# Memory attention with FFN: last quarter of the FFN for the first 384 tokens in float16 halves, later quarters in reverse order

## The chip, the cores and the metric

One core of a Trainium2 chip runs the whole program. The metric is device time in microseconds (us), lower is better; the time before is the median of three runs. A profile is one execution of its own, taken by the hardware profiler; its time is given beside them.

The engines named below are PE (TensorE, matrix products), DVE (VectorE), ACT (ScalarE), POOL (GpSimd) and SP (which issues nearly all transfers). PE reads SBUF and writes PSUM, a memory of eight banks here divided into three pools.

## The reference

Eight batches of eight heads, 576 positions, head size 64. A softmax of `phi` pools keys and values into 32 slots per head; the queries attend to these slots; the result, 4608 tokens of 512 numbers, goes through a feed-forward network (FFN) of width 2048 with a leaky ReLU.

```python
a = softmax(phi, over the 32 slots)               # b h s m
k_m = einsum('bhsm,bhsd->bhmd', a, k)
v_m = einsum('bhsm,bhsd->bhmd', a, v)
attn = softmax(q @ k_m.T / 8)                     # b h s m
x = (attn @ v_m) as (4608, 512)
h = x @ w_in                                      # 512 -> 2048
out = maximum(0.01 * h, h) @ w_out                # 2048 -> 512
```

## The kernel before

**Folding.** `attn @ v_m @ w_in` is computed as `attn @ (v_m @ w_in)`. For each batch b and each quarter j of the FFN's width (four quarters of 512), a fold multiplies the batch's `vT` with the quarter of `w_in` (L1007); the result is the weight of the up products of that batch. So all that PE streams for the FFN is the attention matrix `a` against folded weights (up), and the activated `g` against `w_out` (down).

**Float32 and halves.** A product of float32 operands is one matmul, which the profile shows as two instructions. In halves each operand is split into a float16 high part and a float16 remainder, and a product becomes three matmuls: high x high, remainder x high, high x remainder. The high part is made on ACT (or by a cast on DVE), the remainder by a subtraction on DVE or POOL. The weights arrive as 64-bit numbers and are first rebuilt as float32 (steps `ld`, `h`, `y`, `t`); their scales for halves are known only when all four quarters of `w_in` (`ci.1` to `ci.4`) and of `w_out` (`co.1` to `co.4`) have been squared and summed (`b`).

**Groups and units.** The first 1152 tokens (batches 0 and 1) are done in three groups of 384 tokens, each in eight units: unit u works on quarter u // 2, two blocks of 128 of it (i = 0, 1). A unit's steps are P (up products of a block, PE), V (leaky ReLU, ACT), C and L (the halves of g, DVE), and O (down products of a block into three PSUM tiles, PE). Group 0 (units `u0` to `u7`) runs wholly in float32, before the scales are known, and has no C and L. Groups 1 and 2 (units 8 to 15 and 16 to 23) run in halves. Tokens from 1152 on go through other functions (steps `p`, `v`, `s`, `c`, `l`, `d`, `x`, `z`), which the change doesn't touch.

**Order.** It is written out by hand: `OPENING` and `LATER` are lists of steps, and each step issues its instructions on one engine. On an engine they run in the order of the lists; between engines they wait for data and for buffers to come free. Names of steps used below:

- `a1.*` is the attention of batch 1: `C10` pools keys and values (PE), `C30`, `C31`, `C4` scale them (DVE), `C3k` (ACT), `D10` transposes the keys (PE), `D3` copies them (ACT), `D2` spreads a maximum (PE), `E1` the scores (PE), `E20` to `E22` transpose them (DVE), `Q0`, `Q1` transpose the queries (DVE). `Sc1` to `Sc8` are the softmax of chunk c and its halves, `S02`, `S05`, `S08`, `S12`, `S15`, `S18` of them on POOL.
- `a2.phi` loads phi of batch 2 (SP), `a2.A1` is its maximum and `a2.B10` the subtraction of it (DVE).
- `f0j.1`, `f0j.2`: fold of batch 0, quarter j, in float32 (PE), and its copy to SBUF (ACT). `Wbj.p`: fold for batch b (PE); `Wbj.h0`, `h1`, `l0`, `l1`: its high parts (ACT) and remainders (DVE).
- `oj.k`, `l`: halves of `w_out`, quarter j (ACT, DVE). `oj.s`, `m`, `n`: sums of its blocks for the tokens from 1152 on, and their halves (DVE, ACT, DVE). `ij.k`, `l`: halves of `w_in`.
- `Z0.t`: store of tile t of group 0. `e.`, `e2.`, `osb`: scales (DVE).

The PSUM pool `ps_a` has three banks for everything but the FFN, `ps_h` two for up products, `ps_o` three for down products. A fold takes two banks of `ps_a`, a `co` step one. A load takes the next of eight slots of a ring, or a fixed place, and waits on SP until the last reader of that place is done; what is behind it on SP waits too.

The lines that matter: up products L1091 to L1117, the leaky ReLU L1119, down products L1183 to L1200, stores L1167, folded weights L1042 to L1066, which weight lies in which buffer L309 to L315, the steps of group 0 L1359 to L1389.

Of the kernel before, what the change touches and what calls it, by code (L numbers as in the profile page):

```python
# [45 lines left out]
o1.ld1 u0.P1 a0.S17 i1.y0 o0.t1 u1.V1 i1.h0 i1.h1 i1.y1 i1.t1 u0.V1 i2.ld0 i1.y2 i1.h2 o1.y1 o1.y2
o1.t0 o1.h1 i1.t0 u1.O0 u0.O1 o1.h2 i2.ld1 o2.ld0 i1.t2 f01.1 i2.h0 i2.y0 i2.y1 a0.S18 i2.h1 i2.t1
i2.ld2 f01.2 o2.ld1 o1.t2 o2.ld2 o1.t1 u1.O1 i2.t0 u2.P1 o2.h0 u2.P0 i2.y2 i2.h2 a1.phi o2.y0 i2.t2
o2.t0 a1.kv1 a1.q0 a1.kv0 f02.1 u2.V0 u3.P1 u2.O0 o2.y1 o2.h1 o2.t1 a1.kv2 o2.y2 o2.h2 a1.kv3 a1.A1
u2.V1 u3.P0 o2.t2 i3.ld0 f02.2 a1.q1 a1.A2 a1.A3 u4.P1 a1.B0 u3.V1 u4.P0 a1.B10 u3.V0 i1.b u3.O0  # L50
i2.b u4.V0 a1.B20 u5.P0 a1.B3 o0.b a1.C10 i3.ld2 a1.Q0 i3.ld1 a1.C2 u5.V0 o1.b u2.O1 i3.y0 u5.P1
u4.V1 a1.C30 a1.C31 a1.C3k a1.C4 a1.D10 a1.D2 o2.b i3.h0 a1.D3 a1.Q1 i3.y2 i3.h2 a1.D11 a1.D4 u3.O1
i3.t2 a1.E1 o3.ld0 a1.D5 i3.y1 u4.O0 i3.h1 i3.t0 o3.h0 u5.V1 o3.y0 o3.ld2 u5.O0 a1.E20 i3.t1 a1.E21
i3.b ci.1 o3.ld1 a1.E22 f03.1 a1.S01 a1.S11 a1.S02 a1.S03 a1.S04 u4.O1 o3.y2 o3.y1 o3.h2 ci.2 o3.t0
f03.2 a1.S12 ci.3 ci.4 e. o3.h1 o3.t1 a1.S05 u6.P0 u6.V0 a1.S13 a1.S06 a1.S07 u6.P1 u7.P0 a1.S14
a1.S15 o3.t2 w0.2 u7.V0 u6.O0 a1.S16 o3.b w1.1 co.1 co.2 u7.O0 w1.2 co.3 u6.V1 co.4 u5.O1 o0.k0
# [16 lines left out]
P12.0 o1.m1 O10.0 C11 V12.0 o1.n1 L11 P12.1 o1.s2 O10.1 o1.m2 W03.l1 o1.s3 V12.1 W03.l0 a2.A3 o1.n2
o2.k0 C12 W13.p o2.k2 o2.l0 W13.h1 P13.0 W13.h0 W13.l1 P13.1 W13.l0 V13.0 o2.k1 L12 V13.1 O11.0
o1.m3 P14.0 o2.l1 V14.0 C13 o2.s0 P14.1 L13 o2.m0 O11.1 a2.B10 V14.1 o1.n3 o2.n0 o2.s1 P15.0 a2.B20
C14 o2.m1 O12.0 o2.s2 V15.0 o2.n1 o2.m2 a2.C10 L14 P15.1 o2.s3 a2.B3 O12.1 o2.l2 a2.q0 V15.1 o2.n2
o3.s0 a2.q1 o3.k1 o3.k0 o3.l1 P16.0 P16.1 o3.k2 O13.0 V16.0 C15 o2.m3 o3.s1 O13.1 V16.1 C16 o3.l0
o3.s2 o3.m1 a2.C2 a2.C30 i0.l1 o3.l2 o3.m2 P17.0 L15 o3.m3 o3.n3 O14.0 V17.0 L16 a3.phi P17.1 a2.Q0
# [6 lines left out]
O19.1 i3.k0 W22.p V22.1 a3.A1 i3.k2 L21 a3.A2 W22.h0 P23.0 W22.h1 O20.0 V23.0 a2.S07 P23.1 a3.A4
O20.1 V23.1 a2.S08 i3.l2 C22 i3.l0 W22.l1 C23 W21.l1 O21.0 i3.l1 L23 p0.0 W23.p v0.0 p0.1 W23.h0
p0.2 L22 a3.A3 W23.h1 a3.B10 O21.1 W22.l0 v0.1 a3.B20 W23.l1 a3.C10 O22.0 os2 a3.B3 v0.2 a3.q0
W23.l0 a4.phi a3.C2 p0.3 a3.C30 a3.q1 O22.1 v0.3 a3.C3k s0 c0.0 a3.C31 l0.0 c0.1 a3.D10 l0.1 p1.0
p1.1 a3.D11 v1.0 O23.0 v1.1 a3.C4 p1.2 p1.3 a3.D3 v1.2 a3.Q0 O23.1 v1.3 p2.0 Z2.0 Z2.1 s1 d0.0 Z2.2
p2.1 v2.0 d0.1 v2.1 a3.D2 a4.A1 a3.D4 c1.0 d0.2 c1.1 p2.2 l1.0 d0.3 v2.2 a3.D5 d0.4 a4.A2 p2.3 a4.A4  # L90
# [1403 lines left out]
```

## Time and profile before

| | us |
|---|---|
| median of 3 runs (lowest, highest) | 649.48 (649.35, 651.62) |
| time of the profiled execution | 647.19 |
| its span, first to last instruction | 645.3 |
| PE busy | 632.7 |
| DVE busy | 515.0 |
| ACT busy | 391.2 |
| POOL busy | 29.5 |

The span is what the engines' records cover; the rest of the execution's time lies before its first and after its last instruction. An engine's busy time is the union of its instructions. In a timeline row stand start, length, engine, line of the program, operation, tiles, shapes and count, and in brackets the idle time just before and what ended it; neighbours of one kind are merged. In a view by stretches there are, after the stretch and its length, the busy time of each engine with its number of instructions, the clock granted to TensorE, the DMA engines' busy share and GB/s. A group of instructions has its busy time and mean length in ns, then the idle time before its members. Stretches that matter here: the opening, to about 32 us; group 0, to about 103 us; groups 1 and 2, to about 214 us; the rest.

### The profile page before, as it was taken

To read this page: it belongs to the slowest core of one execution; us is meant where nothing else is said; L and a number is where in the kernel's file an instruction comes from. 1 tells how busy PE (TensorE), PEld (TensorE's weight loads), DVE (VectorE), ACT (ScalarE), POOL (GpSimd) and SP (SyncE) were. 2 spreads that over 40 slices of the span, in tenths; PEclk is the share of its full clock that TensorE was granted. 3 is DMA by queue.
4 is the path that set the end of the run, shared out by engine and by line. 5 is a ranking of instruction groups with operands and counts; after the bars stand their busy time and mean duration, and the time that the engine had idled before them with its cause. 6 is when DMAs were issued, how large, how long until landed. Compare 5 with 4: busy or idle time off the path is not lost.

```text
span 645.3 us, 17189 instructions
## 1 busy us (share of the span) xinstructions
PE 632.7 (98%) x7304; PEld 480.4 (74%) x7304; DVE 515.0 (80%) x863; ACT 391.2 (61%) x671; POOL 29.5 (5%) x37
## 2 busy tenths in 40 slices
PE   6799999999999999999999999999999999999997
...
DMA packets 85501, 61.16 MB, mean 95 GB/s; under 512 B 62000, under 2 KB 68656, under 8 KB 85424
## 3 DMA queue, kind: packets, MB, share of 16 engines
...
q10 hardware_dynamic: 192, 0.13, 0.1%
...
## 4 chain that ended last, share of the span: by engine, by line
PE 94%; DMA 3%; ACT 1%; DVE 1%; issue 0%; SPq 0%; ACTq 0%
PE po L1302 31%; PE ph L1234 22%; PE po L1191 16%; PE ph L1114 8%; PE ph L1302 5%; PE pa L1020 4%; PE pa L698 3%; DMA arena<-in_moe_w_in_dram 2%; PE po L1339 2%; PE pa L861 1%; DMA wo<-in_k_dram 1%; DMA arena<-in_q_dram 0%; ACT arena L397 0%; ACT wi L411 0%; PE pa L887 0%
## 5 line engine op out<-in xcount | busy, mean ns | idle before, releaser
L1302 PEld LDWEIGHTS <-arena 128*128 128x128 f16 x2184 | 209.8, 98 | 31.9 <-issue 8.6
L1250 ACT ACTIVATE wi<-ph,g_sc 128x256 f32<-128x256 f32 (+1 forms) x224 | 98.6, 465 | 160.9 <-PE ph L1234 155.8
L1234 PE MATMUL ph<-a,w_mem 128*128 128x256 f16 (+3 forms) x1440 | 144.8, 246 | 0.1
L1234 PEld LDWEIGHTS <-w_mem 128*128 128x128 f16 x1440 | 114.5, 98 | 13.8 <-issue 3.0
L1302 PE MATMUL po<-wo,arena 128*128 128x256 f16 x936 | 122.1, 273 | 0.0
L1302 PE MATMUL po<-arena 128*128 128x256 f16 x936 | 122.0, 273 | 0.0
L1191 PE MATMUL po<-wo,arena 128*128 128x512 f16 (+1 forms) x384 | 110.3, 433 | 0.0
L1279 DVE TENSOR_TENSOR arena<-arena 128x1024 f16<-128x1024 f32 x52 | 63.5, 1221 | 21.9 <-ACT arena L1275 21.9
L1279 DVE TENSOR_TENSOR arena<-wi,arena 128x768 f16<-128x768 f32 (+1 forms) x60 | 54.7, 911 | 9.5 <-ACT arena L1275 9.5
L1271 DVE TENSOR_TENSOR arena<-wi 128x256 f32<-128x256 f32 x104 | 40.4, 430 | 25.4 <-ACT wi L1250 24.8
L1275 ACT CAST arena<-arena 128x1024 f16<-128x1024 f32 x52 | 54.4, 1046 | 7.9 <-DVE arena L1271 7.6
L1114 PE MATMUL ph<-a,w_mem 128*128 128x192 f16 (+2 forms) x304 | 52.2, 317 | 0.0
L1191 PEld LDWEIGHTS <-arena 128*128 128x128 f16 x288 | 27.9, 98 | 29.6 <-issue 0.6
L1275 ACT CAST arena<-wi 128x768 f16<-128x768 f32 (+1 forms) x60 | 46.6, 776 | 1.5
L1271 DVE TENSOR_TENSOR arena<-wi,arena 128x256 f32<-128x256 f32 x104 | 45.7, 439 | 1.8
L1302 PE MATMUL ph<-wo,arena 128*128 128x256 f16 x312 | 42.6, 273 | 0.0
L985 POOL TENSOR_TENSOR a<-t,a 128x1024 f16<-128x1024 f32 (+2 forms) x16 | 21.9, 1384 | 428.1 <-ACT a L980 428.1
L1191 PEld LDWEIGHTS po<-wo,arena 128*128 128x128 f32 x96 | 17.7, 190 | 20.3 <-issue 18.2
L1020 PE MATMUL pa<-wi,vT 64*32 64x512 f16 (+1 forms) x704 | 28.9, 420 | 1.2 <-ACT vT L805 1.2
L1114 PEld LDWEIGHTS <-w_mem 128*128 128x128 f16 x240 | 20.7, 98 | 10.3 <-issue 4.1
L1121 ACT ACTIVATE arena<-ph,g_sc 128x384 f32<-128x384 f32 x32 | 18.4, 581 | 15.7 <-PE ph L1114 15.4
L1053 ACT ACTIVATE w_mem<-pa 128x512 f16<-128x512 f32 x40 | 22.7, 596 | 7.5 <-PE pa L1020 6.6
...
## 6 DMA issues: line engine op xcount, KB each, us to landing
...
arena<-in_phi_dram SPq DMA_DIRECT2D x7, 576.0 KB, 5.6
arena<-in_q_dram SPq DMA_DIRECT2D x4, 576.0 KB, 8.7
```

Source lines behind the costliest of these rows:

```text
L698: nc.tensor.matmul(var["pk"][g][hh * M:(hh + 1) * M, cs], ld["phi"][rows, hh, j, :], ld["kv", hh][rows, kinds[0]:kinds[-1] + 1, j, :], sta ...
L985: nc.gpsimd.tensor_tensor(piece(lo, tb), piece(t2, tb), piece(hi, tb), ALU.subtract)
L1020: nc.tensor.matmul(pf[g][cols, :], lhs, rhs, start=(n == 0), stop=(n == len(passes) - 1), tile_position=(g * D, hh * M),)
L1053: nc.scalar.activation(tiles(halves(w16(b, j), g)[:, 0]), w(g), AF.Copy, scale=ws)
L1114: nc.tensor.matmul(ph[:, t0:t0 + n * SB], lhs, rhs, start=(m == 0), stop=(m == len(seq) - 1))
L1191: nc.tensor.matmul(po, lhs, rhs, start=(f == 0 and m == 0), stop=(f == NQ * NF - 1 and m == len(seq) - 1),)
L1234: nc.tensor.matmul(ph[:, t0:t0 + n], lhs, rhs, start=(m == 0), stop=(m == len(seq) - 1))
L1250: nc.scalar.activation(dst, ph, AF.Prelu, scale=g_sc2[:, j:j + 1], alpha=SLOPE)
L1271: nc.vector.tensor_tensor(gt[:, x], y, z, op)
L1275: nc.scalar.copy(dst[:, 0], src)
L1279: nc.vector.tensor_tensor(dst[:, 1], src, dst[:, 0], ALU.subtract)
L1302: nc.tensor.matmul(acc, g[:, x, s, u], rhs, start=(h == 0 and j == 0 and u == 0 and m == 0), stop=(j == NQ - 1 and u == 1 and m == 2), ski ...
```

## The change

Quarter 3 of group 0 (units u6 and u7) is computed in halves instead of float32. For that, the first 384 tokens' part of `a` of batch 0 (kept in float32) gets halves of its own (`A0.h` on ACT, `A0.l` on POOL) in a quarter of `w_mem` that held the float32 fold of quarter 3. `f03.1` and `f03.2` go; `W03` is made straight from its fold. Units u6 and u7 get C and L. Quarters 0 to 2 still add up in float32, with another scale, so their sum is set aside (`Y0.t`, ACT), three new tiles take quarter 3, and the store of group 0 scales and adds on DVE.

Groups 1 and 2 go through the quarters in the order 3, 2, 1, 0 (`quarter`), so that the halves of quarter 3, which now exist first, are used first. The halves of `w_out` take the places that come free in that order, and so do the block sums and the folded weights.

`e.` is split by batch, `e2.` leaves out the output scales, which become `os0` and `os1`.

The lists of steps are new from the third unit to the end of group 2; before that PE, DVE and ACT have the same orders, and behind it too, apart from `a7.E1`, which goes behind `p37.3`. The part of the new order that the text below speaks of is shown in the diff.

```diff
@@ OPENING
...
+u5.P0 a1.B3 o0.b a1.C10 i3.ld2 a1.Q0 i3.ld1 a1.C2 u5.V0 o1.b o3.ld0 a1.C30 a1.C31 o2.b u4.V1 u2.O1
+u5.P1 a1.C3k a1.Q1 i3.y0 i3.h0 i3.h2 u3.O1 u5.V1 a1.D10 a2.phi a1.C4 a1.D2 i3.y2 i3.t0 a1.D3 i3.h1
+a1.D4 a1.E1 i3.t2 i3.y1 i3.t1 a1.E20 a1.E22 a1.S01 u4.O0 i3.b ci.1 a2.A1 u5.O0 o3.ld1 o3.ld2 ci.2
+o3.h0 o3.y0 o3.t0 o3.h1 o3.y1 a1.S02 o3.h2 ci.3 u4.O1 a1.E21 ci.4 o3.t1 o3.y2 e0. o3.t2 a1.D11
+a1.S03 a1.S04 e1. a1.S05 a1.S11 a1.D5 W03.p o3.b u5.O1 a1.S06 a2.kv3 W03.h0 A0.h co.1 W03.l0 co.2
+a1.S07 W13.p W03.h1 W13.h0 W03.l1 a2.A2 A0.l co.3 co.4 e2. Y0.0 o3.k1 u7.P1 u7.V1 W13.l0 o3.s0 u6.P1
+a2.A4 W13.h1 u6.P0 os0 u6.V1 o3.m0 u6.V0 o3.k0 a1.S08 W13.l1 o3.s1 o3.n0 Y0.2 u7.P0 u6.C o3.l0 u6.L
+u7.V0 W02.h1 u7.C W12.p o3.k2 W02.h0 o3.l1 P8.1 P8.0 o3.s2 Y0.1 V8.0 u6.O0 V8.1 W02.l0 W02.l1 P9.0
...
+    Q32 = NQ - 1
...
-        [t.bitcast(F16).rearrange("p (i x) -> p i x", i=2) for t in ts[:NQ]] for ts in (wi, wo)
+        [t.bitcast(F16).rearrange("p (i x) -> p i x", i=2) for t in ts]
+        for ts in (wi[:NQ], wo[2:] + wo[:1])
...
-    w_turn = iter([4, 5, 0, 1, 4, 2, 0, 3] + [4, 0, 1, 2, 6, 3] * B)
-    w_of = {(b, j): next(w_turn) for j in range(NQ) for b in range(FB)}
+    w_of = dict(zip([(b, j) for j in range(NQ) for b in range(FB)], (3, 0, 4, 1, 3, 2, 4, 5)))
+    w_turn = iter([4, 3, 2, 1, 6, 0] * B)
...
-        for t in [at(LATE + SUMS * j, SUMS) for j in range(NQ - 1)] + [wo[NQ]]
+        for t in [wo[1]] + [at(LATE + SUMS * j, SUMS) for j in range(NQ - 1)]
...
-            if j == NQ - 1 and x > 0:
+            if j == 0 and x > 0:
...
-    w32 = w_bufs[0:NQ]
+    w32 = w_bufs[0:Q32]
...
-            return tiles(w32[j][g]) if b == 0 else by_tile(src["w"][g])
+            return tiles(w32[j][g]) if b == 0 and j < Q32 else by_tile(src["w"][g])
...
+    def full(G, u):
+
+        return G == 0 and u < 2 * Q32
+
+    def quarter(G, u):
+
+        return u // 2 if G == 0 else NQ - 1 - u // 2
+
+    a0_halves = w_mem[:, 3 * 1024:3 * 1024 + 4 * SB].bitcast(F16).rearrange(
+        "p (tb i g x) -> p tb i g x", tb=2, i=2, g=NG
+    )
+
+    def a0_part(i):
+        src = a_f32(0)[:, 0:2].rearrange("p tb (g x) -> p tb g x", g=NG)
+        hi, lo = a0_halves[:, :, 0], a0_halves[:, :, 1]
+        if i == 0:
+            nc.scalar.copy(hi, src)
+        else:
+            nc.gpsimd.tensor_tensor(lo, src, hi, ALU.subtract)
...
-            a = a_blocks(b)
-            if G == 0:
+            a = a_blocks(b) if G > 0 else a0_halves
+            if full(G, u):
...
-                    (halves(w16(b, f // NF), g)[:, x, fs], a[:, tb:tb + n, y, g, :])
+                    (halves(w16(b, j), g)[:, x, fs], a[:, tb:tb + n, y, g, :])
...
+    def set_aside(t):
+        nc.scalar.activation(obs[:, t * E:(t + 1) * E], pos["32"][t], AF.Copy, scale=1.0 / WT)
+
     def store(G, t, po):
         ob = obs[:, t * E:(t + 1) * E]
-        nc.scalar.activation(ob, po, AF.Copy, scale=row_scale(G, t))
+        if G == 0:
+            nc.vector.scalar_tensor_tensor(ob, po, row_scale(G, t), ob, ALU.mult, ALU.add)
+        else:
+            nc.scalar.activation(ob, po, AF.Copy, scale=row_scale(G, t))
         send(G, t, ob)
...
+        u0, u1 = (0, 2 * Q32) if full(G, u) else (2 * Q32 if G == 0 else 0, NU)
         for m, (lhs, rhs) in enumerate(seq):
             nc.tensor.matmul(
-                po, lhs, rhs, start=(f == 0 and m == 0),
-                stop=(f == NQ * NF - 1 and m == len(seq) - 1),
+                pos["32" if full(G, u) else G][t], lhs, rhs, start=(f == 2 * u0 and m == 0),
+                stop=(f == 2 * u1 - 1 and m == len(seq) - 1),
             )
...
+        if not full(0, u):
+            steps[f"u{u}.C"] = lambda: hi_old(0, u)
+            steps[f"u{u}.L"] = lambda: lo_old(0, u)
```

In the second group the new order on PE is: P8.1, P8.0, u6.O0, P9.0, u6.O1, u7.O0, P9.1, u7.O1, P10.0, W11.p, P10.1, O8.0, P11.0, O8.1, P11.1, O9.0, O9.1, P12.0, W10.p, P12.1, O10.0, O10.1, P13.1, P13.0, O11.0. Before O11.0 DVE has, from u6.L on, the low parts of W02, W12, W01, W11, W00 and one of W10, the block sums of `o3` and `o2` with most of their remainders, the stores of group 0, `a1.S14`, `a2.A3` and `a2.B10`, and C and L of units 7 to 11. In the old order the block sums of `o3` and `o2` come later, and those of `o0` and `o1` stand in their place.

More of the change, by code (lines that the diff above doesn't have):

```diff
@@ L46 @@
[L46 to L56, printed above, removed]
@@ L57 @@
-a1.S08 o0.k1 o0.k2 u7.P1 e2. o0.l0 u7.V1 o0.l1 u6.O1 a1.S17 a1.S18 o0.l2 u7.O1
+a0.C10 i0.ld0 i0.ld1 a0.B3 a0.C2 i0.ld2 z.1 a0.C30 a0.v a0.C3k a0.D10 a0.Q0 a0.D3 a0.E10 a0.Q1 a0.E1
+i0.y0 i0.h0 o0.ld0 i0.t0 a0.E21 z.3 a0.E20 i0.y1 i0.h1 o0.ld2 a0.S01 o0.ld1 o1.ld0 i0.y2 i0.h2 i0.t2
+a0.C11 a0.S02 i0.t1 a0.S03 i0.b a0.E22 a0.S11 a0.C31 o0.y0 a0.D11 a0.S12 a0.D5 f00.1 o0.h0 a0.S04
+i1.ld1 o0.y2 a0.S05 f00.2 a0.S06 a0.C4 z.1 a0.S13 u0.P0 a0.D2 o0.t0 a0.S14 a0.S15 a0.D4 i1.ld0 o0.h1
+u0.V0 o0.y1 u1.P0 u1.P1 o0.h2 u1.V0 o0.t2 i1.ld2 a0.S16 o1.ld2 o1.y0 o1.h0 u0.O0 o1.ld1 u0.P1 a0.S17
@@ L73 @@
[L73 to L78, printed above, removed]
@@ L85 @@
[L85 to L90, printed above, removed]
@@ new lines @@
+W00.l1 o2.n2 o1.s0 O10.0 O10.1 C11 W10.h1 W10.l1 o1.k2 P13.1 L11 o1.m0 P13.0 o2.l2 a2.kv1 C12 O11.0
+O11.1 o1.k0 o1.n0 L12 a2.B3 a2.C10 W10.h0 W10.l0 V13.0 o2.m3 a2.q1 P14.0 V13.1 o1.l0 a2.q0 o2.n3 C13
+o1.l1 a2.C2 a1.S15 V14.0 P15.0 i0.k1 P15.1 O12.0 L13 o1.s1 os1 o1.s2 V15.0 o1.m1 a1.S16 o1.l2 P14.1
+a1.S17 O12.1 o1.n1 V14.1 a2.C30 o1.s3 O13.0 C14 O13.1 a2.C31 L14 o1.m2 V15.1 C15 i0.k0 o1.n2 o0.k0
+o0.l0 a3.phi o0.k2 o0.l2 a1.S18 P16.1 P17.1 V16.1 L15 o0.s0 o0.k1 P17.0 i0.l0 O14.0 V17.0 P16.0
@@ new lines @@
+P23.1 L21 O19.0 o0.n0 P22.0 O19.1 V22.0 i2.k2 i3.k1 i2.l2 P23.0 O20.0 V23.1 P22.1 W21.l0 a2.S06
+V23.0 C23 o1.n3 i3.k2 i3.l2 L23 a2.S07 i3.l1 V22.1 W22.p W22.h1 C22 W22.h0 O20.1 a2.S08 a3.kv2 O21.0
+a3.kv1 i3.k0 i3.l0 W22.l1 W21.h1 W21.l1 a3.A4 p0.0 W23.p v0.0 p0.1 W23.h0 p0.2 L22 a3.A3 W23.h1
+a3.B10 O21.1 W22.l0 v0.1 a3.B20 W23.l1 a3.C10 O22.0 os2 a3.B3 v0.2 a3.q0 W23.l0 a4.phi a3.C2 p0.3
+a3.C30 a3.q1 O22.1 v0.3 a3.C3k s0 c0.0 a3.C31 l0.0 c0.1 a3.D10 l0.1 p1.0 p1.1 a3.D11 v1.0 O23.0 v1.1
+a3.C4 p1.2 p1.3 a3.D3 v1.2 a3.Q0 O23.1 v1.3 p2.0 Z2.0 Z2.1 s1 d0.0 Z2.2 p2.1 v2.0 d0.1 v2.1 a3.D2
@@ new lines @@
+d2.6 a4.B20 d3.0 a3.S07 p5.1 W31.l0 s4 v5.1 a3.S08 d3.1 a4.C10 x3.p a4.q0 c4.0 a4.B3 p5.2 d3.2 c4.1
+d3.3 x3.0 v5.2 d3.4 p5.3 l4.0 v5.3 x3.1 c5.0 l4.1 x3.2 s5 d3.5 d3.6 p6.0 x3.3 p6.1 l5.0 v6.0 d4.0
+p6.2 a4.q1 v6.1 c5.1 d4.1 d4.2 z3.1 a5.phi d4.3 p6.3 l5.1 v6.2 v6.3 d4.4 a4.C2 a4.C30 d4.5 d4.6 p7.0
+p7.1 a4.Q0 d5.0 a4.C3k s6 a4.D10 c6.0 a4.D3 l6.0 v7.0 v7.1 a4.Q1 c6.1 d5.1 a4.C31 d5.2 l6.1 p7.2
+d5.3 v7.2 d5.4 a4.C4 a5.A1 d5.5 d5.6 d6.0 p7.3 p8.0 z3.0 d6.1 a4.E1 a4.E22 d6.2 a4.E3 a5.kv2 v7.3
+v8.0 c7.0 s7 a5.kv0 p8.1 p8.2 v8.1 a4.E20 a5.kv3 c7.1 a4.E21 a4.E23 l7.1 a5.kv1 d6.3 d6.4 p8.3
@@ L1372 @@
         opening(u)
-    for j in range(NQ):
+    for i, key in enumerate("hl"):
+        steps[f"A0.{key}"] = lambda i=i: a0_part(i)
+    for t in range(NT):
+        steps[f"Y0.{t}"] = lambda t=t: set_aside(t)
+    for j in range(Q32):
         def products(j=j):
```

254 lines of the change are left out of this document (122 added, 132 removed).

## Prediction

> **What bounds the kernel now.** I read the page first, then the busy times by stretch, then the chain of waits in order of time.
>
> ```profile
> span 645.3 us, 17189 instructions
> ...
> PE 632.7 (98%) x7304; PEld 480.4 (74%) x7304; DVE 515.0 (80%) x863; ACT 391.2 (61%) x671; POOL 29.5 (5%) x37
> ...
> PE   6799999999999999999999999999999999999997
> ```
> ```profile
> core 0: us, PE busy (x) PEld busy (x) DVE busy (x) ACT busy (x) POOL busy (x), PEclk, DMA share, GB/s
> ...
> 24.00:32.00 8.00, 6.09 (x116) 3.16 (x98) 7.59 (x19) 7.95 (x13) 0.97 (x3) 1.00 1.02 407
> 32.00:40.00 8.00, 8.00 (x23) 3.94 (x22) 5.86 (x10) 7.57 (x14) 2.07 (x3) 1.00 1.03 409
> ...
> 88.00:96.00 8.00, 8.00 (x35) 3.14 (x34) 7.72 (x19) 5.00 (x9) 3.06 (x2) 1.00 0.07 25
> ...
> 112.00:120.00 8.00, 8.00 (x79) 5.40 (x78) 8.00 (x12) 7.35 (x13) 0.00 (x0) 1.00 0.24 70
> 120.00:128.00 8.00, 8.00 (x66) 4.42 (x63) 8.00 (x14) 4.88 (x8) 0.00 (x0) 1.00 0.01 2
> ```
> ```profile
> 67.70:130.30 62.60, 62.60 (x461) 34.00 (x460) 56.44 (x106) 49.12 (x80) 8.16 (x8) 1.00 0.35 111
> ```
>
> TensorE idles only before 32 us: from the row 32:40 on PE is busy 8.00 of 8.00, at clock 1.00. So PE work taken out of the stretch that the change touches is worth its full length, as long as nothing makes PE wait there. The last row is the stretch that decides: PE never waits, but DVE is already busy 56.44 of 62.60 us, and 8.00 of 8.00 between 112 and 128. DVE is the engine that can take PE's place.
>
> **What the change takes off PE.** The chain shows both kinds of step at their real pace.
>
> ```profile
> 31.10 2.58 PE ph L1114 x8
> 33.68 2.57 PE po L1191 x6
> ...
> 116.67 1.94 PE po L1191 x9
> ...
> 144.83 1.95 PE ph L1114 x12
> ```
>
> A down step of the first group in float32 takes 2.57 us (three tiles, each product in two instructions). The same step of a later group in float16 halves takes 1.94 (three tiles, three products each). Two units have four down steps: 4 x 0.63 = 2.52. An up step in float32 is half of the first row, 1.29; in halves (256 + 128 columns in one piece, as in the third group) half of the last, 0.98: 4 x 0.31 = 1.26 with unrounded halves. The fold of quarter 3 is the same sixteen products under another name (f03.1 becomes W03.p): nothing. **PE loses 3.78 us.**
>
> [...]
>
> **What it adds to DVE.** Two casts and two subtractions for units 6 and 7 (C, L), and three stores of the first group that now add on DVE.
>
> ```profile
> L1135 DVE TENSOR_TENSOR arena<-arena 128x768 f16<-128x768 f32 x16 | 15.1, 949 | 0.0
> L1131 DVE CAST arena<-arena 128x768 f16<-128x768 f32 x16 | 8.8, 552 | 2.6 <-ACT arena L1121 2.5
> ...
> L1059 DVE SCALAR_TENSOR_TENSOR w_mem<-pa,w_mem 128x512 f16<-128x512 f32 x8 | 5.3, 684 | 0.0
> ```
>
> 2 x (0.55 + 0.95) + 3 x 0.7 = 5.1 us. The store is not in the trace; the nearest row is the last, same shape, one operand in PSUM, 0.68; with scalars from memory the like costs up to 0.75, so the term lies between 2.0 and 2.3. On ACT the two copies of f03.2 go, one cast (A0.h) comes, and the three stores become three set-asides of the same shape: hidden, since ACT is busy 49.12 of 62.60. If that cover went, it would be under 1 us. POOL gets A0.l; its price stands with the rival on POOL.
>
> **What the new order does to the lead.** In the old order the fourth unit of the second group has its low half (L11) ready long before its first down step (O11.0):
>
> ```profile
> 122.60 0.95 DVE L1135 TENSOR_TENSOR arena<-arena 128x768 f16<-128x768 f32 x1
> ...
> 130.35 2.10 PE L1191 MATMUL po<-wo,arena 128*128 128x512 f16 x9
> ```
>
> That is 130.35 - 123.55 = 6.8 us of lead. For the new order I laid the steps of each engine end to end, each with its own length in this trace (start to start where the engine runs on), the new ones with the rows above, and no waits. DVE, from the end of a1.C31 (67.7) to L11: 82 steps, the first a1.Q1 and the last L11, 59.15 us, so ready at 126.85. PE, from u3.O1 at 68.71 up to O11.0: it arrives at 126.28. The lead is -0.6 us before either has waited once. After P14.0 (lead 0.4) it grows to 1.5 us and more, as the quarters' weights are then ready. So the new order runs DVE and PE level for sixty microseconds, and every wait of DVE there comes out on PE. Three waits can be read off the order.
>
> ```profile
> 16.13 1.15 PE L887 MATMUL pa<-wi,kT 32*32 32x192 f32 x48 [0.67 <-ACT kT L799]
> ```
> ```profile
> 69.14 0.39 PE L344 MATMUL pa<-mdiag,ones 128*128 128x128 f32 x2
> ```
>
> First, a1.D10, a1.D2 and a1.E1 now stand next to one another on PE. E1 needs D3 on ACT, and D3 needs D10. In batch 0, with nothing between, PE idled 0.67 us for this; D2 now covers 0.2 to 0.39. I take 0.4 (between 0.28 and 0.67). Before, a down step of 2.6 us lay between.
>
> ```profile
> 91.23 0.27 PE L471 MATMUL pa<-ident,sq 128*4 128x128 f32 x1
> ```
> ```profile
> 92.49 0.24 DVE L476 TENSOR_REDUCE m<-pa 4x1 f32<-4x128 f32 x1
> ...
> 93.11 0.22 DVE L483 TENSOR_SCALAR diag<-ident,m 4x4 f32<-4x4 f32 x1
> ```
>
> Second, co.1 and W13.p are neighbours on PE. The pool ps_a has three banks: W03.p holds two, co.1 the third. W13.p needs two of them; one comes free by W03.l0, the other only by co.2, four small DVE instructions that read co.1's result (92.49 to 93.33, 0.84 us), and W03.l1 is queued behind co.2. PE waits about 0.27 + 0.84 less the 0.2 that co.1 itself keeps it: 0.9, between 0 (if the bank is free after all) and 1.1. Behind W13.p stand co.3 and the first products of unit 7.
>
> ```profile
> 68.98 1.77 DVE L845 STREAM_TRANSPOSE arena<-arena 96x1536 f32<-96x1536 f32 x1
> ```
> ```profile
> arena<-in_phi_dram SPq DMA_DIRECT2D x1, 576.0 KB, 6.9
> ```
>
> Third, DVE's own waits. a1.E20 waits for the late E1 (0.5). a2.A1 stands some 24 us earlier than before and needs a2.phi, whose load waits for a1.Q1 (now first, ending at 69.4) and took 6.9 us: it lands at 76.3, DVE is there at 75.7, 0.6 us; o3.ld1 and o3.ld2 are queued behind it on SP, which their casts can bear by about a microsecond. co.2 waits for co.1 (0.5). Together 1.6 us, between 0 and 3. With the -0.6 of lead, DVE comes to L11 2.2 us late; PE is 1.3 late by then, so O11.0 waits 0.9 more.
>
> **The sum.** -3.78 + 0.4 + 0.9 + 0.9 = **-1.6 us**; I say -1.5. Against the profiled execution (647.19 us, span 645.3 and 1.9 around it) that is 645.7. The median of the runs shown is 649.48, 2.3 above the profiled one; the change is laid on the median: **648.0 us**. Behind the third group the lists are the same, apart from a7.E1, which changes places with one up step and costs nothing, both being ready.
>
> **Rivals.**
>
> *The whole saving arrives.* If DVE's waits fall where it has its few tenths, and the bank is free for W13.p, all 3.78 stay: 645.7, faster by 0.58%. For it: in the old trace PE waits nowhere after 32 us though some leads were as thin as this (co.3 starts at the very end of the DVE step before it). Against: D10, D3, E1 cannot overlap by their data, whatever the timing. It needs less than 0.5 us given back.
>
> *DVE is blocked by POOL, and the kernel is slower.*
>
> ```profile
> 88.38 3.29 DVE L1059 SCALAR_TENSOR_TENSOR w_mem<-w_mem,ws 128x512 f16<-128x512 f32 x2
> ```
> ```profile
> 88.06 1.74 POOL L945 TENSOR_TENSOR t<-t,ts__901 128x768 f32<-128x768 f32 x1 [7.58 <-ACT w_mem L1053]
> 89.76 1.37 POOL L985 TENSOR_TENSOR a<-t,a 128x384 f16<-128x384 f32 x1
> ```
> ```profile
> L985 POOL TENSOR_TENSOR a<-t,a 128x1024 f16<-128x1024 f32 x6 | 13.5, 2255 | 417.3 <-ACT a L980 417.3
> L985 POOL TENSOR_TENSOR a<-t,a 128x384 f16<-128x384 f32 x4 | 4.6, 1166 | 10.8 <-ACT a L980 10.8
> ...
> L931 POOL TENSOR_TENSOR t<-t,tm 128x768 f32<-128x768 f32 x1 | 1.5, 1480 | 0.0
> ```
>
> Two DVE steps (W00.l0 and l1; their like with an operand in PSUM has 0.68 above) took 3.29 while POOL ran from 88.06 to 91.13: 1.9 us lost in 3.1 of POOL. In the new order POOL's A0.l (1.80 us, between the two L985 rows by size), a1.S08 (1.37), S12 (1.48) and S15 (1.74) all fall where DVE has no slack, 6.4 us. If each blocks DVE for its length, DVE loses 6.4 where my sum holds 1.9 already: O11.0 waits 0.9 + 4.5, the give-back is 6.7 and the time 649.48 + 2.9 = 652.4, slower by 0.45%; with another half microsecond of DVE waits over 0.5%. It turns to a loss once POOL costs DVE 1.6 us more than before. Against: the other POOL steps of the old trace lie beside reductions and transposes and cost DVE nothing, and most of what lies beside them in the new order reads one operand from PSUM. [...]
>
> *The halves don't pay.* If the sixty products in halves (36 down, 24 up) took as long here as the float32 ones, only the waits would be left: 649.5 to 651.7. The rows of 1.94 and 0.98 come from the same shapes with the same weights, so little speaks for it.
>
> **Chances.** Forecast, with 0.6 to 3.4 us given back: 0.56. Whole saving: 0.24. POOL: 0.14, half of it over the line of 0.5%. Halves: 0.06. So faster by over 0.5% (3.25 us, about what a measurement of this kernel can tell from no change): 0.24. Within 0.5%: 0.69. Slower by over 0.5%: 0.07. The forecast's own range is 646.3 to 649.1. The range goes down to the whole saving, 645.3 with the spread of the runs, and up to 651.2: the upper part of the POOL case is left out.
>
> **What would show it.** In the profile after: PE busy down by 3.8 us, 72 float32 instructions left on the line of the down products and 48 on that of the up products; PE idle, so far nothing behind 32 us, in three places: before the scores of a1.E1 about 72 us (0.4), within the fold of W13.p at 86 to 88 (0.9), before the down products of O11.0 near 128 (0.9), each released by ACT or DVE. PE idle 0 behind 32 us would prove the first rival; a DVE step of the fold's low halves, of the sums or of a2.B10 stretched to twice its length beside POOL the second. The forecast is wrong if PE's busy time doesn't fall, or if DVE waits over 3 us between 68 and 126.

## The result and the profile after

| us | before | after |
|---|---|---|
| median of 5 runs, taken in turn on one chip (lowest, highest) | 649.35 (647.61, 651.62) | 654.78 (653.65, 656.23) |
| time of the profiled execution | 647.19 | 656.23 |
| its span | 645.3 | 654.3 |

The ratio is 1.0083, interval 1.0053 to 1.0112: **slower by 0.8%**. The forecast was 648.0, its range 645.3 to 651.2, and 0.07 the chance given to slower by over 0.5%. The profiled execution is the longest of the five.

The page of the kernel after, span, busy times, PE's slices, the clock and the chain:

```profile
span 654.3 us, 17223 instructions
...
PE 632.4 (97%) x7324; PEld 480.1 (73%) x7324; DVE 522.7 (80%) x870; ACT 390.8 (60%) x670; POOL 32.5 (5%) x38
...
PE   6799999999999998999999999999998999999997
...
PEclk9999999999999998999999999999999999999999
...
PE 87%; DVE 5%; DMA 3%; ACT 2%; issue 1%; SPq 1%; ACTq 0%
```

PE's row has two new dents (slices 16 and 31), and the clock one in the first of them. Both lie far behind the steps that were changed. What PE waited for from 32 us on stands in the view of waits (engine, line waited at, what ended the wait: us in total, times, longest); the same question gave no row at all for the kernel before:

```profile
PE pa L700 <- issue: 3.6, 2, 1.9
PE pa L1022 <- DVE w_mem L1061: 1.4, 2, 1.2
PE pa L651 <- DVE r1k L645: 0.8, 1, 0.8
PE pa L491 <- DVE w_mem L1061: 0.7, 1, 0.7
PE ph L1262 <- ACT wi L1278: 0.7, 1, 0.7
PE ph L1135 <- ACT arena L1142: 0.6, 1, 0.6
PE po L1217 <- DVE arena L1156: 0.5, 1, 0.5
PE pa L889 <- ACT kT L801: 0.4, 1, 0.4
```

Eight kinds of wait, 8.7 us, where there was none. The largest is ended by no engine: "issue" is time in which PE waited for nothing that the profile shows. It lies in the pooling of keys and values of batch 4 (`a4.C10`) and of batch 7 (`a7.C10`), steps that the change doesn't touch. PE's timeline at the first, and the stretches around it:

```profile
247.44 2.25 PE L700 MATMUL pa<-arena 64*32 64x128 f32 x139
251.54 0.41 PE L700 MATMUL pa<-arena 64*32 64x128 f32 x5 [1.85 <-issue]
```
```profile
248.00:252.00 4.00, 2.15 (x129) 1.70 (x113) 3.97 (x4) 2.81 (x6) 2.96 (x3) 1.00 0.18 30
252.00:256.00 4.00, 4.00 (x23) 2.88 (x22) 2.40 (x3) 0.47 (x2) 0.00 (x0) 0.57 0.58 90
```

After 139 of 144 products PE stands for 1.85 us, and then runs four us at a mean clock of 0.57 (in the trace's clock record 0.50, from 252.1 to 255.5).

Laid step by step on the kernel before (start of a PE step to the start of the next, so that a wait counts with the step ahead of it), the 8.9 us by which PE ends later are made up like this:

```
opening, to the start of u1.P0                                  +0.67
eight steps of u6 and u7 in halves: down -2.72, up -1.17         -3.89
before a1.B0 (DVE)                                              +0.96
a1.D2, wait before a1.E1 (ACT)                                  +0.61
a1.E1 itself                                                    +0.46
W13.p and wait before co.3 (DVE)                                +1.19
wait before u6.P0 (ACT)                                         +0.74
O11.0 (DVE)                                                     +0.68
p0.0, wait before W23.p (DVE)                                   +1.84
a4.C10 ("issue")                                                +2.10
p5.2, d3.2 and d3.3 at half clock                               +1.65
d13.0 with the wait before p15.2 (ACT)                          +0.58
a7.C10 ("issue")                                                +2.03
all other steps                                                 -0.69
```

So the saving is there to the tenth of a microsecond. Three of the waits were forecast (2.5 us in this list); the rest, over 9 us, was not.

### The profile page after: what moved, and what is told of

Its sections match the earlier page's. It is cut to its first block, busy times and chain, and to the rows that moved or that the text cites. A ratio compares the mean times of both kernels' runs of the same rounds, so it can differ in the third digit from the quotient of the medians.

```text
span 654.3 us, 17223 instructions
## 1 busy us (share of the span) xinstructions
PE 632.4 (97%) x7324; PEld 480.1 (73%) x7324; DVE 522.7 (80%) x870; ACT 390.8 (60%) x670; POOL 32.5 (5%) x38
## 4 chain that ended last, share of the span: by engine, by line
PE 87%; DVE 5%; DMA 3%; ACT 2%; issue 1%; SPq 1%; ACTq 0%
PE po L1330 31%; PE ph L1262 22%; PE po L1217 13%; PE ph L1135 6%; PE ph L1330 5%; PE pa L1022 4%; PE pa L700 3%; DMA arena<-in_moe_w_in_dram 2%; PE po L1367 2%; PE pa L863 1%; DVE w_mem L1061 1%; DVE arena L1156 1%; DMA wo<-in_k_dram 1%; DMA arena<-in_q_dram 0%; DVE wi L423 0%
## 5 line engine op out<-in xcount | busy, mean ns | idle before, releaser
L1330 PEld LDWEIGHTS <-arena 128*128 128x128 f16 x2184 | 210.6, 98 | 32.5 <-issue 8.6
L1262 PEld LDWEIGHTS <-w_mem 128*128 128x128 f16 x1440 | 114.8, 98 | 14.1 <-issue 3.2
L1217 PE MATMUL po<-wo,arena 128*128 128x512 f16 (+1 forms) x396 | 107.4, 419 | 0.5 <-DVE arena L1156 0.5
L1217 PEld LDWEIGHTS <-arena 128*128 128x128 f16 x324 | 31.2, 98 | 34.8 <-DVE arena L1156 1.0
L1135 PE MATMUL ph<-a,w_mem 128*128 128x192 f16 (+2 forms) x288 | 46.9, 307 | 0.0
L1142 ACT ACTIVATE arena<-ph,g_sc 128x384 f32<-128x384 f32 x36 | 20.6, 580 | 24.8 <-PE ph L1135 12.5
L1135 PEld LDWEIGHTS <-w_mem 128*128 128x128 f16 x264 | 23.0, 98 | 13.1 <-issue 4.8
L1022 PE MATMUL pa<-wi,vT 64*32 64x512 f16 (+1 forms) x704 | 29.7, 420 | 2.6 <-DVE w_mem L1061 1.4
L1061 DVE SCALAR_TENSOR_TENSOR w_mem<-pa,w_mem 128x512 f16<-128x512 f32 x40 | 26.3, 679 | 0.6 <-ACT w_mem L1055 0.6
```

Source lines behind the costliest of these rows:

```text
L1022: nc.tensor.matmul(pf[g][cols, :], lhs, rhs, start=(n == 0), stop=(n == len(passes) - 1), tile_position=(g * D, hh * M),)
L1061: nc.vector.scalar_tensor_tensor(tiles(t[:, 1]), w(g), ws, tiles(t[:, 0]), ALU.mult, ALU.subtract)
L1135: nc.tensor.matmul(ph[:, t0:t0 + n * SB], lhs, rhs, start=(m == 0), stop=(m == len(seq) - 1))
L1217: nc.tensor.matmul(pos["32" if full(G, u) else G][t], lhs, rhs, start=(f == 2 * u0 and m == 0), stop=(f == 2 * u1 - 1 and m == len(seq) - 1),)
L1262: nc.tensor.matmul(ph[:, t0:t0 + n], lhs, rhs, start=(m == 0), stop=(m == len(seq) - 1))
L1330: nc.tensor.matmul(acc, g[:, x, s, u], rhs, start=(h == 0 and j == 0 and u == 0 and m == 0), stop=(j == NQ - 1 and u == 1 and m == 2), ski ...
```

## The experiments

The first question is what "issue" stands for. The page of the kernel after has two DMA queues that carry instructions (queue and kind: packets, MB, share):

```profile
q8 instruction: 57, 0.93, 0.6%
q14 instruction: 19, 0.16, 0.1%
```

On q8 that is 57 packets of 16 KB beside PE's 14,730 instructions (with semaphores), 258 to a packet (254 from the start of one packet to that of the next, on the average); q8 is taken as PE's queue, and 256 as what a packet holds. A pooling burst is 288 instructions, 144 weight loads and 144 short products, in some 2.3 us; on the average of the whole span PE needs 13 us for as many. Counting PE's instructions up to the two stalls, by the counts in the view by stretches (PE and PEld; 46 and 76 semaphore instructions come to them):

```profile
0.00:251.50 251.50, 235.89 (x2505) 134.57 (x2506) 218.30 (x355) 161.47 (x260) 20.95 (x27) 1.00 0.52 157
0.00:498.00 498.00, 480.09 (x5690) 344.98 (x5691) 425.13 (x702) 307.33 (x515) 29.83 (x36) 1.00 0.40 114
```

That is 5057 and 11457: 6400 apart, 25 blocks of 256 to the instruction, both the 193rd of their block. **Theory (refill):** a new packet's block begins there. A burst that begins between the 161st and the 193rd meets two such borders, uses up a whole block in 2 us, and the block behind it isn't there yet. The change adds 20 products to PE's stream (each a load and a product) and takes away three semaphore instructions, 37 more in all, so `a4.C10` and `a7.C10`, which began at 132 and 127 of 256, begin at 169 and 164. **Rival:** the loss is the new order's waits, and the stalls have another cause.

### Only the place of the bursts

`e1` and `e2` are the kernel after, `e3` and `e4` the kernel before, with products that nobody reads in the idle step `z.4` of the opening (2 of its 4 idle products taken out in `e1`, `e2` and `e4`).

```diff
+    def padded():
+        pi = ps_a.tile([P, NF, P], F32, name="pa")
+        for _ in range(2):
+            nc.tensor.matmul(
+                pi, ones, ones.unsqueeze(1).broadcast_to([P, NF, P]), start=True, stop=True
+            )
+        for _ in range(56):
+            nc.tensor.matmul(pi[:32, 0, :2], ones[:32, :32], ones[:32, :2], start=True, stop=True)
...
+    steps["z.4"] = padded
```

> The kernel after, with 216 more PE instructions in the opening, where PE waits for the first loads anyway (two of the four idle products out, 56 products of 32x2 in). It shifts the place of every later PE instruction in its 256-instruction block: the two stalling bursts (a4.C10, a7.C10) start at 129 and 124 of 256 instead of 169 and 164, the other bursts between 51 and 240. Refill theory: the stalls of 1.9 and 1.7 us and the half clock of 3.4 us between them go, nothing else changes: 5.8 us less, 649.0 us (647.5 to 650), the same as before within 0.3%. Rival (the new order's waits or another cause make the stalls): no change, 654 to 656 us with both stalls in place.

> The kernel after, with exactly 256 more PE instructions at the same place, so that every later instruction keeps its place in its block. Refill theory: nothing changes against the kernel after, 654.8 us (653.5 to 656.5), both stalls at the 193rd of 256. Rival (extra instructions in the opening by themselves move the time): as the run with 216.

> The kernel before, with 40 more PE instructions in the opening (10 products of 32x2), the number by which the change lengthens PE's stream: a4.C10 and a7.C10 now start at 172 and 167 of 256. Refill theory: both bursts stall as in the kernel after, 1.7 to 2.1 us each, with a spell of half clock after the first: 5 to 6 us more than before, 654.5 to 655.5 us, ratio 1.008. Rival: no change, 649.4 us.

> The kernel before with 256 more PE instructions in the opening, places in the blocks unchanged. Both theories: no change, 649.4 us within 0.2%; a longer time would be the price of the added products themselves, to be taken off the other three.

| | median, us | ratio to before (interval) | start of u1.P0 | u1.P0 to PE's end, against before |
|---|---|---|---|---|
| before (profiled) | 649.33 | | 30.94 | 604.49 |
| after (profiled) | 654.78 | 1.0083 | 31.61 | +8.25 |
| e1: after + 216 | 652.83 | 1.0062 (1.0043 to 1.0081) | 34.01 | +1.73 |
| e2: after + 256 | 657.92 | 1.0134 (1.0115 to 1.0152) | 36.16 | +5.94 |
| e3: before + 40 | 653.79 | 1.0068 (1.0051 to 1.0084) | 33.68 | +3.89 |
| e4: before + 256 | 652.20 | 1.0049 (1.0033 to 1.0064) | 34.36 | +0.63 |

The last column runs from the start of u1.P0 to the start of PE's last group of 54 products, which takes 6.06 us in before and in after. The medians of `e1`, `e2` and `e4` lie 2.8 to 3.8 us above their forecasts, that of `e3` 0.7 below: the products in the opening are not free, as `e4` says. The clock granted in the first 32 us was lower too, 0.84, 0.68, 0.89 and 0.84 in the profiles of `e1` to `e4` against 1.00 in before and after; but two runs of `e4` with a mean clock of 1.000 took 652.17 and 652.70 us, so the clock alone is not it. The last column leaves the opening out, and there the theory holds. The stalls go with 216 and stay with 256; in the kernel before they appear with 40:

```profile
246.99 2.25 PE L698 MATMUL pa<-arena 64*32 64x128 f32 x138
250.50 0.42 PE L698 MATMUL pa<-arena 64*32 64x128 f32 x6 [1.26 <-issue]
```

This is `a4.C10` of `e3`, the kernel before with ten more tiny products 240 us earlier. Its two bursts stalled 1.26 and 1.73 us, those of `e2` 1.55 and 1.90, those of after 1.85 and 1.73: six bursts that began at 164 to 172, each stalled at the 193rd instruction of a block. Bursts that began elsewhere passed, behind the opening, in all six kernels. One place speaks against so simple a rule: `a2.C10` begins at 167 in before and `e4` and passed with a gap of 0.2 us. Its packet began 0.2 us ahead of the burst; in after it began 1.2 us (`a4`) and 1.9 us (`a7`) behind its start. Why it came earlier there stays open. `e3` has one other wait far behind the opening, 0.8 us for ACT before p15.2, the same that the list for after has with 0.58; since its lists are the old ones, that wait is not the new order's. In `e2` and `e3` the clock stayed 1.00 behind all four stalls, so the 1.65 us at half clock belong to one stall in six, and to this profile rather than to the median.

### The bursts in two parts

The cure would be shorter bursts. `e5` to `e8` cut `a4.C10` and `a7.C10` into 160 and 128 instructions and put other products between.

```diff
+            cut = 5 if b in (4, 7) else KJ
+            steps[f"{name}C10"] = lambda: slots_of((0, 1), range(cut))
+            steps[f"{name}C11"] = lambda: slots_of((0, 1), range(cut, KJ))
...
-d3.3 x3.0 v5.2 d3.4 p5.3 l4.0
+d3.3 x3.0 v5.2 d3.4 p5.3 a4.C11 l4.0
...
-a7.B3 d33.4 a7.q0 a7.C2
+a7.B3 d33.4 a7.q0 a7.C11 a7.C2
```

> The kernel after with two bursts of 288 PE instructions (a4.C10, a7.C10) issued in two parts, 160 and 128, with 60 to 90 other PE instructions (three to four us) between; no instruction added. Refill theory: no stall and no half clock is left, 5.8 us less than after: 649.0 us (648 to 650), the same as before. Rival (the stalls come from what stands around these bursts, not from their length against the 256 instructions of a block): the stalls stay, 654 us.

> As e5, and the subtraction L23 (949 ns alone, 2.89 us in the kernel after) moved on DVE from beside POOL's a2.S08 to ahead of L22, where POOL is idle, as in the kernel before. POOL theory: L23 falls to 0.95 us, W22.l1 and W21.l1 come about 1.9 us earlier, PE's wait of 1.2 us before W23.p falls to 0.3 or less: 1.0 to 1.5 us less than e5, 647.6 us. Rival (the wait at W23.p is the new order's own, whatever L23 takes): the wait stays over 0.9 us, the time within 0.4 us of e5.

> As e6, and two PE waits filled: u4.P1 goes back ahead of a1.B0 (0.96 us in the kernel after), and u3.O1 stands between a1.D10 and a1.E1 (0.5 to 1.0 us). Both are to vanish at their places. If DVE sets the pace from there to O11.0, as the prediction had it, PE only arrives earlier at later waits: those before co.3, u6.P0 and O11.0 grow by 1 us or more together and the time falls by 0.5 us or less against e6. Rival (PE sets the pace): the whole 1.5 us arrive.

> As e7, and on DVE C11 and L11 moved up behind a2.B10 (4 us earlier, ahead of work that is needed later), on ACT u7.V1 ahead of o3.k1. If the lead of L11 is what cost the wait at O11.0, that wait goes to zero, and the gains of e7 arrive: 1.5 to 2.5 us less than e6, 645.5 us; the remaining give-back against the 3.8 us saved is then the wait before co.3 alone. Rival: another DVE result is late next (O12.0, P14.0, O13.0), and the time stays within 0.5 us of e7.

Measured: 663.43, 664.70, 663.90 and 663.72 us. The cut was put in the wrong place: the lists are also the order in which buffers are used, and `a4.q0` and `a7.q0` stand between the two parts. So the second part reads q where k and v had been, and waits for that load (in `e7` 7.0 us for `in_q_dram` in all). These four times answer nothing. Their steps ahead of 246 us are unharmed, and three things can be read there. `e6`, L23 moved: the wait at the fold L1022 falls from 1.4 to 0.5 us.

```profile
PE pa L1024 <- DVE w_mem L1063: 0.5, 2, 0.3
```

`e7`, PE's waits filled: those before `a1.B0` and `a1.E1` are gone from the view of waits, PE is 1.5 us earlier on its way, and yet the later ones stay as they were, O11.0's among them:

```profile
PE pa L491 <- DVE w_mem L1063: 0.7, 1, 0.7
...
PE ph L1137 <- ACT arena L1144: 0.6, 1, 0.6
...
PE po L1219 <- DVE arena L1158: 0.5, 1, 0.5
```

So DVE did not set the pace there: it had itself been waiting for PE (its wait for `a1.C10` at 64 us, 2.2 us in after, is 1.2 in `e7`). `e8`: with C11 and L11 earlier the wait of O11.0 is gone (2.62 to 1.94 us), but `u7.V1` ahead of `o3.k1` makes `u6.P0` 0.8 us worse, and was given up.

`s5` is `e5` with `a4.q0` and `a7.q0` behind the second part; `s6` adds the order mends of `e7` and `e8` that had worked, `s8` two more.

```diff
-a1.A3 a1.B0 u3.V1 u4.P1 a1.B10
+a1.A3 u4.P1 a1.B0 u3.V1 a1.B10
...
-i3.h2 u3.O1 u5.V1 a1.D10 a2.phi
+i3.h2 u5.V1 a1.D10 u3.O1 a2.phi
...
-a2.B10 W00.l0 P12.1
+a2.B10 C11 L11 W00.l0 P12.1
```

> The kernel after with the bursts a4.C10 and a7.C10 in two parts as in e5, but the loads a4.q0 and a7.q0 (which write over what the second part reads) behind the second part. Nothing else differs from after. Refill theory: no wait on 'issue' of over 0.3 us in either part, clock 1.00 throughout, 5.8 us less than after: 649.0 us (648 to 650), within 0.2% of before. Rival (the loss of the change is the new order's waits): 653 us or more.

> As s5, with three of the order's waits mended: u4.P1 back ahead of a1.B0, u3.O1 between a1.D10 and a1.E1, C11 and L11 behind a2.B10. By the PE steps of e7 and e8 these give 0.96, 0.95 and 0.68 us, and nothing behind them grows: 2.6 us less than s5, 646.4 us (645.5 to 647.5), 0.3 to 0.6% faster than before. If they only move the wait to the next DVE result: less than 1 us.

> As s6, with L23 behind a3.B10 (so neither beside POOL's a2.S08 nor ahead of a3.A3), and W03.h1 and W03.l1 ahead of A0.h and co.2, so that the bank that co.3 needs is free earlier. W23.p's wait falls from 1.4 to 0.5 us and that before co.3 from 0.7 to 0.2: 1.2 us less than s6, 645.2 us (644.2 to 646.5), faster than before by 0.5 to 0.8%. Rival for L23: what is queued on DVE behind a3.B10 (W22.l0, W23.l1) comes late for p0.3 and c0.0, and the gain is under 0.5 us.

Measured: 654.97 (ratio 1.0089, 1.0069 to 1.0109), 653.28 (1.0067, 1.0042 to 1.0093) and 653.52 (1.0071, 1.0046 to 1.0096). In `s5` the stalls are gone at both places: 4.45 us of `a4.C10` become 1.48 + 1.09, 4.60 of `a7.C10` 1.69 + 1.09. But q comes late now: `a7.E1` takes 2.91 us instead of 1.17, `d6.2` 1.61 instead of 0.76, and `p5.3` waits 0.7 us for ACT. The cure cost what it brought, by a chain of its own; so `s5` by its time alone would have spoken for the rival. `s6` against `s5` shows the mends at their places (-0.96, -0.52, -0.68) and 1.7 us in the median where 2.6 were expected. `s8` gained 0.87 at W23.p, lost 0.60 at u6.P1 (the wait before u6.P0, with which the section on the prediction deals) and 0.49 at `a3.C10`.

### The place alone, without a price

What was open by then: is the time gone too, or only moved? `t1` is the kernel after, with 28 short products (112 instructions) where PE waits for DVE anyway, ahead of `co.3`. They go to the PSUM tile that `u7.P1` then writes over.

```diff
+    spare = {}
+
+    def padded():
+        ph = spare[0, 7, 1] = ps_h.tile([P, GT], F32, name="ph")
+        for x in range(28):
+            rows = slice(x % 4 * 32, x % 4 * 32 + 32)
+            nc.tensor.matmul(
+                ph[rows, 0:64], ones[0:64, 0:32], ones[0:64, 0:64], start=True, stop=True,
+                tile_position=(0, x % 4 * 32),
+            )
...
-a2.A2 A0.l co.3 co.4
+a2.A2 A0.l z.9 co.3 co.4
```

`t2` adds the three mends shown for `s6`; `t3` to that L23 behind `a3.B10`; `t4` instead, to `t2`, `A0.h` and `A0.l` behind `a1.S03`, and `W03.h1`, `W03.l1` ahead of `co.2`.

> The kernel after with 28 short products (32x64 from 64 rows, 112 PE instructions, 0.85 us at the pace of the bursts) on PE ahead of co.3, where it waits 0.7 us for DVE anyway. Their result is written over. Every burst behind starts 112 later in its block of 256: a4.C10 at 25, a7.C10 at 20, a5.C10 at 136, the others from 224 to 230. Refill theory: neither burst stalls, clock 1.00 throughout, 5.8 us less than after and at most 0.3 us for the products: 649.2 us (648.2 to 650.2), ratio to before 0.999 to 1.002. Rival (what is gained there comes back as another wait): 653 us or more.

> As t1, and the three order mends of s6 (u4.P1 ahead of a1.B0, u3.O1 between a1.D10 and a1.E1, C11 and L11 behind a2.B10). By the steps of s6 against s5 they give 2.5 us: 646.7 us (645.7 to 647.7), ratio to before 0.994 to 0.997. Rival (they only bring PE earlier to waits on DVE or ACT): within 1 us of t1.

> As t2, and L23 behind a3.B10, out of POOL's a2.S08. W23.p's wait falls by 0.9 us, of which a3.C10 gives back about 0.5 (by s8): 0.4 us less than t2, 646.3 us (645.2 to 647.4), ratio to before 0.993 to 0.997. Rival (no part of it arrives): t2 within 0.1 us.

> As t2, and A0.h and A0.l (cast and subtraction of the a blocks for units 6 and 7) behind a1.S03, some 4 us earlier, where ACT stands idle, so that POOL does not run beside co.2; and W03.h1 and W03.l1 ahead of co.2, so that the bank that co.3 needs comes free about 1 us earlier. If POOL stretched co.2: its four steps fall from 1.2 us to 0.75. If the bank is what holds PE there: the waits in W13.p and before co.3 (0.3 and 0.7 us) fall to 0.3 together; the short products then cost up to 0.6 us of it. Time 0.2 to 0.8 us less than t2, 648.3 us, ratio to before 0.996 to 0.999. Rival (the next wait, of u6.P0 for u7.V1, takes it up): PE at P8.1 within 0.2 us of t2.

| | median, us | ratio to before (interval) | u1.P0 to PE's end, against before |
|---|---|---|---|
| t1 | 650.53 | 1.0012 (0.9996 to 1.0029) | +1.90 |
| t2 | 648.78 | 0.9983 (0.9968 to 0.9997) | -0.07 |
| t3 | 648.68 | 0.9988 (0.9970 to 1.0007) | +1.01 |
| t4 | 648.37 | 0.9999 (0.9981 to 1.0018) | +0.28 |

`t1` settles the first question: nothing but the place of the bursts is changed, and 4.25 of the 5.4 us go (654.78 to 650.53; the 0.85 us of short products didn't fit wholly into the wait, and `a5.C10`, which now begins at 135, costs 0.5 us of "issue" 21 instructions behind its end, again at the 193rd of a block). PE's waits from 32 us on:

```profile
PE pa L1022 <- DVE w_mem L1061: 1.4, 2, 1.2
PE ph L1148 <- ACT arena L1155: 0.6, 1, 0.6
...
PE po L1343 <- issue: 0.5, 1, 0.5
PE pa L889 <- ACT kT L801: 0.4, 1, 0.4
```

`t2` takes the order's own waits: 1.75 us less than `t1` (2.5 expected), and the first version whose ratio lies under 1, by 0.17% with an interval that just leaves 1 out. That is weak: the medians of `t2` and of the runs of before beside it, 648.78 and 649.06, are 0.04% apart. So the loss is made good, and that `t2` is faster than before is not shown. `t3` and `t4` cannot be told from it. In `t3` L23 falls from 2.89 to 0.95 us and W23.p comes earlier, but `a3.C10` then waits 0.4 us for its exponentials on ACT: what was gained on one engine is late on the next.

The median of `t4` is the one forecast, its ratio isn't (0.9999 for 0.996 to 0.999), and it missed its reason: `co.2` did not fall to 0.75 us but rose to 1.75. With `A0.l` out of the way, POOL's `a1.S08` and `a1.S12` ran beside it instead, and where `A0.l` now stood, `a1.S04` took 2.12 us instead of 0.95. Against `t2` PE gained 0.63 us all the same, since the wait before u6.P0 is gone; at 330 us it lost 0.72 to the wait before p15.2 that `e3` has too.

```profile
PE ph L1275 <- ACT wi L1291: 0.6, 1, 0.6
```

## Why the prediction was right and wrong

**The saving.** Right: 3.78 forecast, 3.89 measured (the down steps -0.63 to -0.73 each, the up steps about -0.3), and the counts are the ones named:

```profile
L1217 PE MATMUL po<-wo,arena 128*128 128x512 f32 x72 | 33.1, 598 | 0.0
L1135 PE MATMUL ph<-a,w_mem 128*128 128x384 f32 x48 | 17.2, 492 | 0.0
```

PE's busy time fell by 0.3 us alone, where 3.8 had been named as the sign. 1.65 us of the difference are the products at half clock and 0.46 a1.E1; another 2.0 are the edges of the waits: the steps that hold them grew by 10.7 us in the list, of which the view of waits has 8.7 as idle, so that the rest counts as busy.

**The wait before a1.E1.** Right: 0.4 forecast, 0.45 measured, on ACT, and gone with `u3.O1` in between. That `a1.E1` itself took 2.31 instead of 1.86 us is not the order's: in `t1`, with the same order, it took 1.86.

**The wait at W13.p.** Right in size, 0.9 forecast and 1.1 measured, and in its cause, the bank behind `co.2`; but most of it stands a step later, 0.68 us before `co.3`, and W13.p itself takes 0.44 more than in the kernel before (the second view).

```profile
89.06 1.53 PE L1022 MATMUL pa<-wi,vT 64*32 64x512 f32 x16
...
91.27 0.35 PE L491 MATMUL pa<-diag,ones 4*128 4x4 f32 x2 [0.68 <-DVE w_mem L1061]
```
```profile
90.21 1.09 PE L1020 MATMUL pa<-wi,vT 64*32 64x512 f32 x16
```

Part of it is a stretch that was not in the sum. The steps of `co.2` and the POOL instruction beside them:

```profile
89.17 0.28 DVE L478 TENSOR_REDUCE m<-pa 4x1 f32<-4x128 f32 x1 [0.37 <-PE pa L473]
89.48 0.14 DVE L479 TENSOR_SCALAR m<-m 4x1 f32<-4x1 f32 x1
89.66 0.14 DVE L480 TENSOR_SCALAR m<-m 4x1 uint32<-4x1 uint32 x1
89.83 0.63 DVE L485 TENSOR_SCALAR diag<-ident,m 4x4 f32<-4x4 f32 x1
90.39 0.73 DVE L1061 SCALAR_TENSOR_TENSOR w_mem<-pa,ws,w_mem 128x512 f16<-128x512 f32 x1
```
```profile
88.81 1.64 POOL L1104 TENSOR_TENSOR w_mem<-a,w_mem 128x768 f16<-128x768 f32 x1 [2.25 <-ACT w_mem L1102]
```

W13.p gets its bank when L478 has read `co.1`; `co.3` waits for the one that L1061 (W03.l1) frees, behind `co.2`, whose last step took 0.63 us on a 4x4 tile, against 0.22 in the kernel before.

**The wait before O11.0.** Right in place, 0.5 against 0.9, but for a reason that fell. The prediction laid DVE's and PE's steps end to end and found them level for sixty microseconds, so that "every wait of DVE there comes out on PE". By `e7` PE can come 1.5 us earlier and O11.0 waits no longer than in after: DVE comes earlier with it. The wait came from where L11 stood in DVE's list, behind five DVE steps that could wait; with L11 moved up, it is gone (`e8`, `t2`). Two of the five, W00.l0 and W00.l1, took 2.62 us beside POOL's `a1.S15`, and 1.41 in `t2`, where they lie behind it; the prediction's sum held that price with its row of 3.29.

**DVE's own waits.** Wrong in detail: 1.6 us forecast, 2.4 in the view of waits between 68 and 126 us. `a1.E20` waited 0.2 for the scores and `co.2` 0.4, near the 0.5 each that had been named; for a2.phi DVE waited not at all, and instead 0.8 for the high half of a fold on ACT, 0.7 for a load of `w_in` and 0.3 more for ACT. With all short gaps DVE was idle for 3.6 us there (busy 54.36 of 58.00), over the 3 that the prediction had named as a sign against itself.

**Where the step failed: "Behind the third group the lists are the same", so nothing was charged there.** Two losses have no need of a changed list. The first is the stall of the bursts: 4.1 us (2.10 + 2.03) in after and 4.0 in `e2`, the two profiles that kept this order's places (1.8 to 2.2 us each), and 1.65 more in after, where the clock stood at 0.50 for 3.4 us behind the first. None of the rivals held it. The trace of before did: its packets on the instruction queue, its bursts of 288, and `a2.C10` with its 0.2 us at the same border.

The second is W23.p, inside the stretch whose order is new. The prediction checked DVE's lead up to L11, wrote that after P14.0 it grows, and looked no further. L23 and POOL's `a2.S08` in the kernel after:

```profile
194.99 2.89 DVE L1156 TENSOR_TENSOR arena<-arena 128x768 f16<-128x768 f32 x1
```
```profile
194.47 3.69 POOL L987 TENSOR_TENSOR a<-t,a 128x1024 f16<-128x1024 f32 x2 [47.71 <-ACT a L982]
```

The same subtraction takes 0.95 us alone. This is the rival "DVE is blocked by POOL", right in kind and price (1.9 us); it was bounded for the steps up to O11.0 and came again behind them. Up to O11.0 POOL held DVE for 2.3 us (0.41 in `co.2`, 0.67 in `co.4`, 1.2 in W00.l0), little more than the 1.9 that the sum held, but the first two now stand in PE's way. The new order brought this subtraction beside a POOL step that had lain beside DVE's idle time. By `t3` and `s8` its cure is worth 0.2 to 0.4 us here, not 1.4, since ACT is late next.

**Not seen at all:** 0.96 us before `a1.B0`. The end-to-end count began at 67.7 us, behind `a1.C31`, while the lists are new from about 55 us on; there `a1.B0` had moved ahead of `u4.P1`, which covered the DVE step it needs. And 0.74 us before `u6.P0`: four up steps in a row share two banks of `ps_h`, and `u7.V1`, which frees one, stood behind `o3.k1` on ACT. `o3.k1` in turn needs the scale that `co.4` makes, and its last step, L496, ran beside POOL's `a1.S12` and to its end. After, before, and the chain of waits after:

```profile
91.28 1.48 POOL L933 TENSOR_TENSOR t<-t,tm 128x768 f32<-128x768 f32 x1
...
91.94 0.84 DVE L496 TENSOR_SCALAR sw<-sw 128x4 f32<-128x4 f32 x1
```
```profile
94.83 0.17 DVE L494 TENSOR_SCALAR sw<-sw 128x4 f32<-128x4 f32 x1
```
```profile
91.94 0.85 DVE sw L496
92.79 0.02 issue
92.82 0.73 ACT wo L418
93.55 0.11 issue
93.66 0.57 ACT arena L1142
94.23 0.04 issue
94.27 2.18 PE ph L1135 x12
```

In `t4` POOL is not beside it, L496 takes 0.17 us, and the wait before u6.P0 is gone. In `s8` POOL's `a1.S12` meets the next small step instead, a product on 128x4 tiles (L503), which takes 1.47 us instead of 0.15, and the wait is 1.20 us. Other steps were moved in both runs as well, but in all three the wait goes with the length of this chain.

**The other rivals.** "The whole saving arrives" fell with the eight kinds of wait; "the halves don't pay" with the first point.

**What is left.** `t2` has neither stalls nor the three mended waits, saves the same 3.9 us, and yet stands at -0.07 in its body: W23.p 1.84, W13.p and `co.3` 1.2, `u6.P0` 0.74 still stand and give back 3.8 between them. All three stand behind a DVE step that POOL held (L23 2.88 us, `co.2`'s last 0.64, `co.4`'s last 0.81). No run frees all three at once, so what the change would bring without them stays open. The single profiles differ by up to 3 us in the opening (u1.P0 begins at 31.6 us in after, 32.7 in `t1` and 34.8 in `t2`, with the same steps ahead of it and 1.00, 0.89 and 0.73 of the clock granted in the first 32 us), so no gain under half a microsecond was settled by a profile's span. The medians mix such executions: of the 29 of the kernel before beside `t1` to `t3`, the nine with a mean clock of 0.999 or more took 647.85 us on average and the other twenty 649.95.
